# Row gradients as full-array block-diagonal products, fixed tiles for column vectors, gathered gradient tails, and a new order, in a planned attention-and-MLP gradient kernel

## The chip, the cores and the metric

The kernel runs on one core of a Trainium2 chip. A core has five engines with an instruction queue each: TensorE (PE, with its weight loads shown apart as PEld), VectorE (DVE), ScalarE (ACT), GpSimd (POOL) and SyncE (SP), and 16 DMA engines that move data between HBM and the on-chip memory SBUF. PE writes its products to PSUM; ACT and DVE copy them from there to SBUF, and a DMA stores them. The metric is the device time of one execution in microseconds (us). Before the change it is 470.13 us, the median of three runs (469.51 to 470.38).

## The reference

One token for each of two batch rows passes a layer norm, then attention over a cache of 4,096 positions and, in parallel, a gated bilinear MLP. The kernel computes the output and the gradients of all inputs but one:

```python
xn = _layernorm(x)                                   # (2, 1, 576)
q = xn @ wq                                          # 32 query heads of 128
scores = einsum("bhqd,bhkd->bhqk", q, k) * Dh**-0.5  # 16 cache heads, two query heads on each
o = softmax(scores) @ v
A = o @ wo
B = ((xn @ w_gate) * (xn @ w_up)) @ w_down           # 576 -> 4608 -> 576
out = x + A + B
_out, _vjp = jax.vjp(_f, A_x, A_k_cache, A_v_cache, A_wq, A_wo, B_w_gate, B_w_up, B_w_down)
return (_out, *_vjp(grad_out))
```

All arrays are bfloat16. The outputs are `out_0` (the result), `out_1` (gradient of x), `out_2` and `out_3` (gradients of the k and v caches, 32 MB each), `out_4` (of wq, 576 x 4096), `out_5` (of wo, 4096 x 576), `out_6` and `out_7` (of w_gate and w_up, 576 x 4608) and `out_8` (of w_down, 4608 x 576). With one token and a batch of two, every weight gradient is a sum of two outer products, and every cache gradient is one outer product for each pair of query heads. There is therefore little arithmetic for each byte: 92.5 MB are read and 92.5 MB are written.

## The kernel before

**Tiling.** Caches are worked on in 16 steps, each with two of the 16 cache heads and one batch row; each step loads two 1 MB buffers of k (t = 0) and two of v (t = 1). Weights are worked on in groups of 512 columns or rows: 8 groups for wq and wo, 9 slices for the MLP. All the large data goes through 16 SBUF buffers called `big` (128 partitions x 4,096 bfloat16), shared by cache loads (`kv`, at most 6), turned copies (`X`, 10), stores (`st`, 5) and the MLP's two weights (`G`, 2). PSUM gives three double-bank tiles `o` for outer products and two banks `m` for everything else.

**One step.** A loaded cache buffer is turned on DVE in 32 x 32 blocks (`t32`, L465), multiplied with the query (`score`, L1267), and passes softmax or its gradient. The probabilities are spread, and `contract` (L1441) sums the cache rows. GpSimd builds a block-diagonal tile `BD` (L1255) from a query or gradient vector, and `head_outer` (L1289) multiplies it with the spread probabilities: four products-and-copies of 1,024 columns fill one 1 MB store. The copy from PSUM is `cp`, on ACT (L469) or on DVE (L471).

**Weight gradients.** Three helpers make them, each through `unit` (take an `o` tile, multiply, copy to a store buffer, set an event) and `put` (wait for the events, start the store on SP, L695):

- Rows (`rows_unit`, `rows_outer`, L720 to L741) serve `out_5` and `out_8`. A vector tile `t` holds four blocks of 32 partitions that stand for four sets of gradient rows. Each of four units issues eight products of 32 partitions by 32 by 288 columns, one for each quadrant of the array, and one copy of 576 columns. Its event, on which `hb` or `R` is given back, comes when all four copies are done.
- Columns (`wide_unit`, `wide_outer`, L756 to L785, and `cols_unit` for a single slice) serve the first 512 rows of `out_4`, `out_6` and `out_7`, for three or four slices at a time. Each slice's vectors lie in a ring tile of their own (`D`, five of them; `Q`, six), so that a unit issues one product of 128 columns for each slice and each of two row groups.
- Tails (`tail_outer`, L813 to L835) serve rows 512 to 575, one slice at a time, through two small buffers `tl`: two copies of 256 columns, and a store of 64 rows of 1,024 bytes for each output.

**The order.** No order is written out by hand. All parts are Python generators, and the class `Order` plays them against estimated costs: at each turn it lets the part with the best due time go on, and the instructions come out in that sequence. Due times come from `pr(name, s)`: a step width, a constant for each kind of work (`PR`), corrections for the first and last steps (`HEAD`, `TAIL`) and one for each kind and step (`OFF`). `MLP_AT`, `WQ_AT` and `WO_AT` say behind which cache load the weights' loads come. So every engine's sequence is fixed when the kernel is built. SP issues all loads and nearly all stores in one sequence, and a store at its head that waits for a copy holds back every transfer behind it.

Of the kernel before, what the change touches and what calls it, by code (L numbers as in the profile page):

```python
# [13 lines left out]
P = 128  # L14
# [236 lines left out]
def DVE(cost):  # L251
    return ("op", "DVE", cost)
# [38 lines left out]
def DMA(engine, cost, nbytes, row=8192):  # L291
# [6 lines left out]
CAP = {"kv": 6, "X": 10, "st": 5, "G": 2}  # L298
OFF = {"mload": {0: 271.6, 1: -102.6, 2: -55.0, 3: -1.2, 4: 302.0, 5: -37.8, 6: -3.1, 7: -261.9, 8: -10.9, 10: 33.1,
       11: 0.8, 12: -207.4, 13: 133.1, 14: -7.7, 15: 159.7}, "wload": {0: 133.7, 1: 303.1, 2: 22.2, 3: 90.3,  # L300
# [7 lines left out]
       11: 190.3, 12: -28.6, 13: -116.3, 14: -697.9, 15: 68.4}, "load": {0: 14.2, 1: -78.4, 2: 45.7, 3: 100.8,  # L308
       4: -197.6, 5: 28.3, 6: 554.3, 7: 177.4, 8: 2.5, 9: -143.0, 10: -2.3, 11: -21.3, 12: 8.4, 13: -73.3, 14: 100.6,
       15: -142.0}, "front": {0: -179.7, 1: 85.4, 2: -277.2, 3: -256.2, 4: 1826.5, 5: 49.9, 6: 24.7, 7: 68.7,  # L310
       8: 74.6, 9: -133.5, 10: 299.2, 12: -72.9, 14: -82.2}, "turn0": {0: -74.5, 1: 12.8, 2: -59.7, 4: -98.2,
       5: -13.7, 6: 27.8, 7: -195.0, 8: 25.3, 9: -324.6, 10: 62.5, 11: 150.3, 12: 36.5, 13: 374.6, 14: 6.0,
       15: 40.1}, "con": {0: -246.4, 1: 1581.7, 2: 912.6, 3: -19.4, 4: -192.0, 5: -376.3, 6: -83.8, 8: 66.8,
       9: -106.8, 10: 1369.4, 12: 147.6, 13: 65.7, 14: 198.1, 15: 79.0}, "W0": {0: 31.7, 1: -255.2, 2: 62.9,
       3: -322.1, 4: -90.7, 5: -152.2, 6: 579.2, 7: -124.9, 8: 27.6, 9: -89.0, 10: -18.9, 11: -62.1, 13: 324.8,
       14: 5.0, 15: 14.0}, "back": {0: -32.5, 1: 35.1, 2: -23.7, 3: -119.2, 4: 97.7, 5: 800.9, 6: -2327.5, 9: -276.5,
# [3 lines left out]
       9: -447.4, 10: 31.8, 11: -210.3, 12: -58.4, 13: -249.2, 14: -11.7, 15: 118.0}, "dsc": {0: -165.3, 2: -11.7,  # L320
       3: -436.2, 4: 52.6, 5: -31.9, 7: 88.0, 8: -832.8, 9: 9.9, 10: -27.9, 12: -325.8, 14: 576.3, 15: -5.7},
       "mlp": {0: 894.9, 1: 15.9, 3: -552.7, 4: -163.6, 5: -290.8, 6: 30.0, 7: -24.7, 9: -5.3, 10: -0.7, 11: -155.0,
       12: -3.1, 13: 1.8, 14: 185.9, 15: 66.1}, "att": {0: 223.1, 1: 245.8, 2: -323.8, 4: 2.7, 5: -249.3, 7: -26.2,
       8: -319.6, 9: -120.7, 10: -196.9, 11: -385.5, 12: -86.1, 13: 62.5, 14: 3.3, 15: -375.0}, "conv": {1: 35.5,
       2: 158.9, 3: 36.7, 4: 96.9, 5: -12.0, 6: 28.4, 7: 88.3, 9: 84.0, 10: 537.9, 11: -9.1, 12: -109.0, 13: 291.0,
       14: 0.9, 15: 65.7}}
MLP_AT = [1.54, 11.84, 12.88, 7.42, 26.87, 116.29, 33.85, 48.49, 96.78]
WQ_AT = [-22, 9, 14, 22, 14, 17, 46, 47]
WO_AT = [-45, -45, -9, -46, 33, 37, 23, 31]
# [6 lines left out]
HEAD = {"turn0": -123.1, "turn1": -2289.3, "att": -2854.2, "dsc": -818.2, "con": 709.7, "out1": -2234.5,  # L336
        "out0": 965.3, "front": 1154.9, "back": -1312.3, "W0": 566.4, "W1": -1455.9, "BD1": 458.6, "BD0": 2899.0,
        "conv": -1146.6, "load": -3357.2}
TAIL = {"turn0": 905.5, "turn1": 2241.7, "att": -614.0, "dsc": -353.2, "con": 2724.6, "conv": 1530.3, "out1": 5670.9,
        "out0": -405.8, "front": -274.2, "back": 1989.7, "W1": 1283.8, "BD1": -1838.9, "BD0": -790.0, "load": 134.3,  # L340
        "W0": 1916.8}
PR = {"turn0": 854.2, "turn1": 1429.3, "att": -2428.5, "dsc": -1571.7, "conv": 280.9, "con": -1020.5, "out1": 3897.0,
      "out0": 1865.4, "front": 130.7, "back": 822.0, "W0": -2573.1, "W1": 268.5, "BD1": 2424.3, "BD0": -1416.8,
      "mlp": -908.1, "wout": -411.3, "store": -2408.5, "load": -294.1, "wload": -4334.0, "fin": -803.5,
      "const": 5061.6, "mload": -1458.5}
# [8 lines left out]
def kernel(  # L354
# [63 lines left out]
    tl_t = tiles("tl", 2, [P, FS])  # L418
# [4 lines left out]
    D_t = tiles("D", 5, [P, 2, P])  # L423
# [11 lines left out]
    Q_t = tiles("Q", 6, [P, P])  # L435
# [5 lines left out]
    for i in range(2):  # L441
        ch_t.append(dict(
            mx=const.tile([P, 1], FP32, name=f"mx{i}"), m4=const.tile([1, 4], FP32, name=f"m4{i}"),
            mr=const.tile([1, P], FP32, name=f"mr{i}"),
            negb=const.tile([P, 1], FP32, name=f"negb{i}"), ex=const.tile([P, P], FP32, name=f"ex{i}"),
            z=const.tile([P, 1], FP32, name=f"z{i}"), rz=const.tile([P, 1], FP32, name=f"rz{i}"),
            pr=const.tile([P, P], BF16, name=f"pr{i}"), cs=const.tile([P, 1], FP32, name=f"cs{i}"),
            cr=const.tile([P, 1], FP32, name=f"cr{i}"), ds=const.tile([P, P], BF16, name=f"ds{i}"),
            sp=const.tile([P, 2 * P], BF16, name=f"sp{i}")))

# [48 lines left out]
    xi = filled("xi", [2, 2, P], BF16, 0.0)  # L499
# [20 lines left out]
    mask16 = const.tile([P, 16], BF16, name="mask16")  # L520
    fold = const.tile([P, 4, GH], BF16, name="fold")
# [7 lines left out]
    def consts():  # L529
# [22 lines left out]
        yield DVE(0.45)  # L552
        sums(Q4[:], [[32, 4], [1, 32]])
        nc.vector.tensor_copy(mask8[:], view(Q4[:], 0, P, 0, [[1, 4], [0, 2]]))
# [12 lines left out]
    xnb = const.tile([2, D], BF16, name="xnb")  # L567
# [30 lines left out]
    def front():  # L598
# [16 lines left out]
        nc.vector.tensor_scalar(xnb[:], xb, mv[:, 0:1], rstd[:], op0=ALU.subtract, op1=ALU.mult)  # L615
# [4 lines left out]
        nc.vector.tensor_copy(view(xi[:], 0, 2, 0, [[P + 1, 2], [2, 64]]), view(xnb[:], 0, 2, 512, [[0, 2], [1, 64]]))  # L620
# [99 lines left out]
    def rows_unit(j, t, st):  # L720
        A, k = divmod(j, 2)

        def mms(o):
            for aa in range(2):
                for q in range(4):
                    nc.tensor.matmul(o[32 * q:32 * q + 32, aa, 0:HD2], lhsT=view(t, 32 * q, 32, 2 * A + aa, [[4, 32]]),  # L726
                                     rhs=dyr[32 * q:32 * q + 32, k * HD2:(k + 1) * HD2], start=True, stop=True)

        def ev(e, o):
            cp(e, view(st[:], 0, P, 2 * A * D + k * HD2, [[D, 2], [1, HD2]]), o[:, :, 0:HD2])  # L730
        return mms, (0.12, 0.208), D, ev

    def rows_outer(t, dst, p, event):
        i = yield ACQ("st")
        st, done = st_t[i], events(FC)
# [5 lines left out]
        yield SET(event)  # L741
# [14 lines left out]
    def wide_unit(rhss, dc, A, st, off):  # L756
        n = len(rhss)

        def mms(o):
            for j, rhs in enumerate(rhss):  # L760
                for aa in range(2):
                    a = 2 * A + aa
                    nc.tensor.matmul(o[:, aa, j * P:(j + 1) * P], lhsT=xnr[32 * a:32 * a + 32, dc * P:(dc + 1) * P],  # L763
                                     rhs=rhs(a), start=True, stop=True)
# [4 lines left out]
        return mms, (0.053 * n, 0.052 * n), 2 * P * n, ev  # L769

    def wide_outer(rhss, dst, p, event):
        width, last = FS * len(rhss), []
# [14 lines left out]
    def release(tag, slots, wait):  # L787
        yield WAIT(*wait)
        for i in slots:
            yield REL(tag, i)  # L790
# [801 lines left out]
```

## Time and profile before

| | |
|---|---|
| median of three runs | 470.13 us (469.51 to 470.38) |
| profiled execution: span from first to last instruction | 465.4 us (the profile gives no other time for it) |
| PE, DVE, ACT, POOL busy | 372.3, 372.8, 333.6, 143.2 us |
| data moved, mean rate | 185.97 MB, 400 GB/s |
| DMA issues | 26 of 64 KB from `tl`, 17 of 576 KB, 74 of 1 MB and 5 of 512 or 768 KB from `big`, 2 of the result rows; the rest are loads |
| mean granted TensorE clock | 0.715 |

"Busy" is the time in which an engine executed something; copies that overlap at their ends count once. The page cuts the span into 40 slices and gives for each how busy the DMA engines were and how many GB/s they moved. A group of instructions is named by its line, engine, operation and the tiles that it writes and reads; its row gives the busy time, the mean of one instruction in ns, and the idle time of its engine just ahead of it, with what ended that idle time. In the list of SP's waits the three numbers are the sum in us, how many waits, and the longest one.

### The profile page before, as it was taken

The numbers are of one execution on the slowest core, as the hardware profiler recorded it, in microseconds if no ns is written. First come the engines' busy times: TensorE is split into PE (matmuls) and PEld (weight loads), VectorE is DVE, ScalarE is ACT, GpSimd is POOL, SyncE is SP. The second block draws the span as 40 slices with busy tenths as digits, with TensorE's granted clock in tenths as the row PEclk, the third lists the DMA queues.
The fourth block names the chain that finished last, engine by engine and source line by source line (L and its number), as shares of the span: only waits on it lengthen the run. The fifth ranks groups of instructions, "written<-read, shape, count | busy, mean of one in ns | idle before, by whom it ended". The sixth has DMA issues, their size and how long they took to land.

```text
span 465.4 us, 15712 instructions
## 1 busy us (share of the span) xinstructions
PE 372.3 (80%) x6750; PEld 213.0 (46%) x6750; DVE 372.8 (80%) x711; ACT 333.6 (72%) x512; POOL 143.2 (31%) x174
## 2 busy tenths in 40 slices
PE   1688779888987777888788877789788978977886
PEld 1545355546443344455555354455424533544443
DVE  8887888878779787879887778788878866877883
ACT  3268638969986687675777775678778968687874
POOL 0740042403407343470015341600743316033200
PEclk9997675877776677677775696756866665677865
DMA  8999999999999999999999999999999999999995
GB/s 316 414 410 420 411 421 387 417 416 373 371 422 422 405 424 406 420 420 421 413 407 419 419 417 404 400 350 374 418 422 424 418 411 424 423 359 390 422 368 207
DMA packets 40710, 185.97 MB, mean 400 GB/s; under 512 B 3640, under 2 KB 12352, under 8 KB 24256
## 3 DMA queue, kind: packets, MB, share of 16 engines
q1 hardware_dynamic: 40632, 184.96, 98.7%
q8 instruction: 53, 0.87, 0.7%
q14 instruction: 17, 0.14, 0.1%
q10 hardware_dynamic: 8, 0.00, 0.0%
HBM read 92.48 MB, written 92.48 MB: 397 GB/s over the span
## 4 chain that ended last, share of the span: by engine, by line
DMA 35%; PE 20%; ACT 10%; DVE 10%; issue 5%; SPq 1%; DVEq 0%; ACTq 0%
DMA out_dram<-big 20%; DMA big<-in_A_v_cache_dram 15%; ACT big L469 8%; DVE big L465 6%; PE ps_o L1289 4%; PE ps_m L1441 3%; PE ps_m L1267 3%; PE ps_o L726 2%; DVE big L471 2%; PE ps_o L763 1%; PE ps_m L677 1%; SPq L1197 1%; PE ps_m L887 1%; ACT pr L1357 0%; PE ps_o L1539 0%
## 5 line engine op out<-in xcount | busy, mean ns | idle before, releaser
L469 ACT CAST big<-ps_o 128x1024 bf16<-128x1024 f32 (+2 forms) x303 | 272.5, 957 | 51.0 <-PE ps_o L1289 31.4
L465 DVE STREAM_TRANSPOSE big<-big 128x1024 f32<-128x1024 f32 x146 | 176.3, 1223 | 21.6 <-DMA big<-in_A_v_cache_dram 10.1
L1255 POOL TENSOR_TENSOR BD<-vr,mask 128x2048 bf16<-128x2048 bf16 x32 | 115.3, 3603 | 118.6 <-PE ps_o L1289 42.9
L471 DVE CAST big<-ps_o 128x1024 bf16<-128x1024 f32 (+1 forms) x75 | 81.3, 1086 | 15.6 <-PE ps_o L1289 5.9
L1267 PE MATMUL ps_m<-big,W 128*32 128x128 bf16 x2048 | 60.2, 281 | 5.4 <-issue 3.5
L1232 POOL COPY W<-rep 32x16 bf16<-32x16 bf16 x128 | 24.5, 192 | 116.7 <-DVE rep L1006 95.8
L1267 PEld LDWEIGHTS <-W 128*32 128x32 bf16 x2048 | 47.0, 125 | 24.8 <-issue 23.7
L1289 PE MATMUL ps_o<-BD,pp 32*128 32x512 bf16 x256 | 46.1, 495 | 12.9 <-ACT big L469 7.2
L1289 PE MATMUL ps_o<-BD,dd 32*128 32x512 bf16 x256 | 43.6, 499 | 9.9 <-ACT big L469 7.8
L465 DVE STREAM_TRANSPOSE big<-ww 128x1152 f32<-128x1152 f32 (+1 forms) x25 | 33.0, 1319 | 2.4 <-DMA out_dram<-big 1.1
L1441 PE MATMUL ps_m<-big,pp 128*32 128x512 bf16 x256 | 31.9, 582 | 3.5 <-DVE pp L465 3.2
L1441 PE MATMUL ps_m<-big,dd 128*32 128x512 bf16 x256 | 28.3, 533 | 1.7 <-DVE dd L465 1.4
L1289 PEld LDWEIGHTS <-pp 32*128 32x128 bf16 x256 | 10.2, 97 | 33.2 <-issue 24.6
L1289 PEld LDWEIGHTS <-dd 32*128 32x128 bf16 x256 | 10.5, 98 | 24.8 <-issue 16.9
L1038 POOL COPY qr<-qd 128x256 bf16<-128x256 bf16 x8 | 3.2, 396 | 54.2 <-DVE qd L471 43.8
L726 PE MATMUL ps_o<-dyr,R 32*32 32x288 bf16 x256 | 18.0, 401 | 1.6 <-ACT big L469 1.5
L763 PEld LDWEIGHTS <-xnr 32*128 32x128 bf16 x368 | 12.5, 117 | 10.7 <-issue 9.2
L726 PE MATMUL ps_o<-dyr,hb 32*32 32x288 bf16 x288 | 15.5, 330 | 1.3 <-ACT big L469 1.2
L887 PE MATMUL ps_m<-big,Wdy 128*128 128x128 bf16 x162 | 15.0, 265 | 0.2
L763 PE MATMUL ps_o<-D,xnr 32*128 32x128 bf16 x256 | 13.3, 276 | 2.3 <-ACT big L469 1.7
L677 PE MATMUL ps_m<-big,wm 128*32 128x128 bf16 x416 | 13.4, 290 | 1.5 <-DVE qd L992 0.8
L1451 ACT ACTIVATE osb<-ps_m 128x512 bf16<-128x512 f32 x15 | 9.0, 597 | 7.9 <-PE ps_m L1441 7.7
(205 smaller groups left out, 483.8 us busy)
## 6 DMA issues: line engine op xcount, KB each, us to landing
out_dram<-big SPq DMA_DIRECT2D x74, 1024.0 KB, 14.0
big<-in_A_k_cache_dram SPq DMA_DIRECT2D x32, 1024.0 KB, 14.4
big<-in_A_v_cache_dram SPq DMA_DIRECT2D x32, 1024.0 KB, 12.6
out_dram<-big SPq DMA_DIRECT2D x17, 576.0 KB, 10.7
ww<-in_B_w_down_dram SPq DMA_DIRECT2D x9, 576.0 KB, 12.2
ww<-in_A_wo_dram SPq DMA_DIRECT2D x8, 576.0 KB, 7.4
ww<-in_A_wq_dram SPq DMA_DIRECT2D x8, 512.0 KB, 12.4
big<-in_B_w_gate_dram SPq DMA_DIRECT2D x4, 1024.0 KB, 14.6
```

The lines of the kernel that those rows point to most:

```text
L465: nc.vector.transpose(out, in_)
L469: nc.scalar.copy(out, in_)
L471: nc.vector.tensor_copy(out=out, in_=in_)
L677: nc.tensor.matmul(dp[32 * q:32 * q + 32, 0:P], lhsT=W, rhs=view(X, 0, P, xoff(q, s), [[FS, 4], [2, 32]]), start=(s == 0), stop=(s == S - 1))
L726: nc.tensor.matmul(o[32 * q:32 * q + 32, aa, 0:HD2], lhsT=view(t, 32 * q, 32, 2 * A + aa, [[4, 32]]), rhs=dyr[32 * q:32 * q + 32, k * HD2: ...
L763: nc.tensor.matmul(o[:, aa, j * P:(j + 1) * P], lhsT=xnr[32 * a:32 * a + 32, dc * P:(dc + 1) * P], rhs=rhs(a), start=True, stop=True)
L887: nc.tensor.matmul(dh, lhsT=Wdy[:, e, 2 * k:2 * k + P], rhs=view(X[:], 0, P, 64 * k + e, [[D, FC], [2, 32]]), start=(k == 0 and e == 0), s ...
L1232: nc.gpsimd.tensor_copy(view(W_t[t][w][:], 32 * a, 32, 6 + 8 * a, [[G * WW, 4], [WW, G], [1, 2]]), view(rep_t[grp[g]["qs"]][:], 32 * a, 32 ...
L1255: nc.gpsimd.tensor_tensor(BD_t[i][:], view(vr_t[v][:], 0, P, 0, [[0, 16], [1, Dh]]), view(mask16[:], 0, P, 0, [[1, 16], [0, Dh]]), ALU.mult)
L1267: nc.tensor.matmul(sc[32 * cq:32 * cq + 32, :], lhsT=view(W[:], 0, P, (be * G + l) * WW + 6 - 4 * c2 - 2 * l, [[1, 32]]), rhs=view(X[:], 0 ...
L1289: nc.tensor.matmul(o[:, k, :], lhsT=pr2[32 * c4:32 * c4 + 32, :], rhs=BD[32 * c4:32 * c4 + 32, 8 * l + 4 * h2:8 * l + 4 * h2 + 4, :], star ...
L1441: nc.tensor.matmul(ct[32 * j:32 * j + 32, :], lhsT=view(rT, 0, P, 4 * c + 2 * l, [[1, 32]]), rhs=kv_t[kvS[s][t][l]][:, Dh * c:Dh * (c + 4) ...
```

## The change

- **Rows.** GpSimd expands the vector tile into `RB`, a tile of 4 x 128 columns in which each block of 32 partitions keeps only its own 32 columns and is zero elsewhere (a product with the mask `maskq`). One product over all 128 partitions then gives what took four quadrants before. The row gradient is treated as one flat stretch of 2,304 columns that is cut at 1,024 and 2,048 for the copies, and for the products also at multiples of 512 and 576: 3, 4 and 1 products and one copy each. The event that gives `hb` or `R` back now comes behind `RB`'s construction.
- **Columns.** The ring tiles `D` and `Q` become fixed tiles `Dm` (nine slices) and `Qm` (eight groups). Slices lie side by side, so one product covers up to four of them. Nothing is given back any more.
- **Tails.** They are gathered: MLP slices 0 to 3 and 4 to 8 for both outputs, groups 0 to 3, 4 to 6 and 7 for `out_4`. They take an `st` buffer of `big` instead of `tl`, and a store has rows of 1,024 bytes for each slice gathered.
- **Memory.** To make room, the helper tiles `xi`, `xnb` and `mr` lie inside `Dm` and `sp`.
- **Order.** All constants of `pr`, `OFF`, `HEAD`, `TAIL`, `MLP_AT`, `WQ_AT`, `WO_AT`, and also `BIAS` and `SLACK`, have new values, so every engine's sequence is new. The last cache loads, for example, have 24 transfers behind them on SP instead of 25.

```diff
-BIAS = 0.186
-SLACK = {"PE": 0.09, "ACT": 0.26, "DVE": 0.4, "POOL": 5392037994838238.0, "SP": 5703748027825.79}
+BIAS = 0.255
+SLACK = {"PE": 0.03, "ACT": 0.26, "DVE": 0.37, "POOL": 10000.0, "SP": 10000.0}
...
-    tl_t = tiles("tl", 2, [P, FS])
-    D_t = tiles("D", 5, [P, 2, P])
+    RB_t = tiles("RB", 2, [P, 4, P])
+    Dm = const.tile([P, NFS, 2, P], BF16, name="Dm")
+    Qm = const.tile([P, NG, P], BF16, name="Qm")
-    Q_t = tiles("Q", 6, [P, P])
...
-    def rows_unit(j, t, st):
-        A, k = divmod(j, 2)
+    def rows_unit(RB, lo, hi, st):
+        cuts = sorted({lo, hi} | {x for x in range(lo, hi) if x % FS == 0 or x % D == 0})
 
         def mms(o):
-            for aa in range(2):
-                for q in range(4):
-                    nc.tensor.matmul(o[32 * q:32 * q + 32, aa, 0:HD2], lhsT=view(t, 32 * q, 32, 2 * A + aa, [[4, 32]]),
-                                     rhs=dyr[32 * q:32 * q + 32, k * HD2:(k + 1) * HD2], start=True, stop=True)
+            flat = o[:].rearrange("p a n -> p (a n)")
+            for x, y in zip(cuts, cuts[1:]):
+                c, n = divmod(x, D)
+                nc.tensor.matmul(flat[:, x - lo:y - lo], lhsT=RB[:, c, :], rhs=dyr[:, n:n + y - x], start=True, stop=True)
...
     def rows_outer(t, dst, p, event):
+        b = yield ACQ("RB")
+        RB = RB_t[b]
+        yield POOL(0.95)
+        nc.gpsimd.tensor_tensor(RB[:].rearrange("p c (q m) -> p c q m", q=4), view(t, 0, P, 0, [[1, 4], [0, 4], [4, 32]]),
+                                view(maskq[:], 0, P, 0, [[0, 4], [1, 4], [0, 32]]), ALU.mult)
+        yield SET(event)
...
-        for j in range(FC):
-            yield SPAWN(unit(*rows_unit(j, t, st), done[j]), p)
+        for u in range(3):
+            yield SPAWN(unit(*rows_unit(RB, 1024 * u, min(1024 * u + 1024, FC * D), st), done[u], kind="f"), p)
...
-    def wide_unit(rhss, dc, A, st, off):
+    def wide_unit(n, rhs, dc, A, st, off):
         def mms(o):
-            for j, rhs in enumerate(rhss):
-                for aa in range(2):
-                    a = 2 * A + aa
-                    nc.tensor.matmul(o[:, aa, j * P:(j + 1) * P], lhsT=xnr[32 * a:32 * a + 32, dc * P:(dc + 1) * P],
-                                     rhs=rhs(a), start=True, stop=True)
+            for aa in range(2):
+                a = 2 * A + aa
+                nc.tensor.matmul(o[:, aa, 0:n * P], lhsT=xnr[32 * a:32 * a + 32, dc * P:(dc + 1) * P],
+                                 rhs=rhs(a), start=True, stop=True)
...
-    def tail_outer(rhss, dsts, p, event, w0=0):
-        i = yield ACQ("tl")
+    def tail_outer(n, rhss, dsts, p):
+        i = yield ACQ("st")
+        st, parts = st_t[i], [(j, min(j + 4, n)) for j in range(0, n, 4)]
...
+    BUNCH, TAILS = ((0, 1, 2, 3), (4, 5, 6, 7), (8,)), ((0, 1, 2, 3), (4, 5, 6, 7, 8))
```

More of the change, by code (lines that the diff above doesn't have):

```diff
@@ L566 @@
     xy = const.tile([2, 2 * D], BF16, name="xy")
-    xnb = const.tile([2, D], BF16, name="xnb")
+    xnb = view(Dm[:], 0, 2, 0, [[1, D]])
     bst = const.tile([2, 2, 6], FP32, name="bst")
@@ L828, in ev @@
             def ev(e, o):
-                r = slice(64 * w0, 64 * (w0 + nw))
-                cp(e, st[r, 256 * A:256 * A + 256].rearrange("p (a f) -> p a f", a=2), o[r, :, 0:P])
-            return mms, (0.053, 0.104), 256, ev
-        for A in range(2):
-            yield SPAWN(unit(*mk(A), done[A]), p)
-        yield WAIT(*done)
-        yield SET(event)
+                r = slice(0, 64 * nw)
+                cp(e, view(st[:], 0, 64 * nw, FS * j0 + 2 * P * A, [[P, 2], [FS, j1 - j0], [1, P]]),
+                   o[r, :, 0:P * (j1 - j0)].rearrange("p a (j f) -> p a j f", j=j1 - j0))
@@ new lines, in mk, with bunch_outer @@
+            return mms, (0.053 * (j1 - j0), 0.052 * nw), 2 * P * (j1 - j0), ev
+        for k, (j0, j1) in enumerate(parts):
+            for A in range(2):
+                yield SPAWN(unit(*mk(A, j0, j1), done[2 * k + A]), p)
+    def bunch_outer(gs, p):
+        g0, g1 = gs[0], gs[-1] + 1
+        if len(gs) > 1:
+            yield SPAWN(wide_outer(g1 - g0, lambda a: Qm[32 * a:32 * a + 32, g0:g1, :], out_4[0:512, g0 * FS:g1 * FS], p), p)
+        else:
+            yield SPAWN(cols_outer(lambda a: Qm[32 * a:32 * a + 32, g0, :], out_4[0:512, g0 * FS:g1 * FS], p, Event()), p)
+        yield SPAWN(tail_outer(g1 - g0, [lambda a, j0, j1: Qm[32 * a:32 * a + 32, g0 + j0:g0 + j1, :]],
+                               [out_4[512:576, g0 * FS:g1 * FS]], p), p)
@@ new lines, with grads @@
+    BUNCH, TAILS = ((0, 1, 2, 3), (4, 5, 6, 7), (8,)), ((0, 1, 2, 3), (4, 5, 6, 7, 8))
+    dE = [Event() for _ in range(NFS)]
+    def grads(ks, p):
+        yield WAIT(*[dE[k] for k in ks])
+        k0, k1 = ks[0], ks[-1] + 1
+        for w, out in enumerate((out_6, out_7)):
+            dst = out[0:512, k0 * FS:k1 * FS]
+            if len(ks) > 1:
+                yield SPAWN(wide_outer(k1 - k0, lambda a, w=w: Dm[32 * a:32 * a + 32, k0:k1, w, :], dst, p), p)
+            else:
+                yield SPAWN(cols_outer(lambda a, w=w: Dm[32 * a:32 * a + 32, k0, w, :], dst, p, Event()), p)
@@ L837, in free_gu, with tail_grads @@
+    def tail_grads(ks, p):
+        yield WAIT(*[dE[k] for k in ks])
+        k0, k1 = ks[0], ks[-1] + 1
+        yield SPAWN(tail_outer(k1 - k0, [lambda a, j0, j1, w=w: Dm[32 * a:32 * a + 32, k0 + j0:k0 + j1, w, :] for w in range(2)],
+                               [out[512:576, k0 * FS:k1 * FS] for out in (out_6, out_7)], p), p)
     def free_gu(sl):
@@ L904, in mlp @@
         yield SPAWN(rows_outer(hb[:], out_8[f0:f0 + FS, :], po, E[0]), po)
-        yield SPAWN(tail_outer([lambda a, w=w: D2[32 * a:32 * a + 32, w, :] for w in range(2)],
-                               [out[512:576, f0:f0 + FS] for out in (out_6, out_7)], po, dE[i][1]), po)
-        for ks in BUNCH:
-            if i == ks[-1]:
-                yield SPAWN(grads(ks, po), po)
+        for todo, kss in ((grads, BUNCH), (tail_grads, TAILS)):
+            for ks in kss:
+                if i == ks[-1]:
+                    yield SPAWN(todo(ks, po), po)
         yield DVE(0.31)
```

160 lines of the change are left out of this document (65 added, 95 removed), and 21 rows, old and new, of the table OFF.

## The prediction

> **What bounds the kernel now.** I read the page's busy shares and DMA queue first, then the DMA queue's own waits, then stretches of the span, then the groups of instructions by shape.
>
> The page:
>
> ```profile
> PE 372.3 (80%) x6750; PEld 213.0 (46%) x6750; DVE 372.8 (80%) x711; ACT 333.6 (72%) x512; POOL 143.2 (31%) x174
> ...
> DMA  8999999999999999999999999999999999999995
> GB/s 316 414 410 420 411 421 387 417 416 373 371 422 422 405 424 406 420 420 421 413 407 419 419 417 404 400 350 374 418 422 424 418 411 424 423 359 390 422 368 207
> ...
> q1 hardware_dynamic: 40632, 184.96, 98.7%
> ```
>
> The one DMA queue has packets under way for nearly the whole span, but a slice moves between 350 and 424 GB/s. The trace's packet records give the floor: taken at the median time of their size (309 ns for 8,192 bytes, 178 for 4,608, 159 for 4,096, 121 for 3,072, 46 for 1,024, 9 for the completion write that each DMA leaves on each of 16 engines), all data packets make 446.1 us of sixteen engines. The span is 465.4, so 19.3 us are lost. By the same records about 2.6 go at the start and 3 to 5 behind the last cache load; the remaining 11 or so lie between.
>
> The DMA queue's own waits, and five stretches (PE, PEld, DVE, ACT, POOL busy, clock, DMA share, GB/s):
>
> ```profile
> SPq L695 <- ACT big L469: 81.7, 48, 4.8
> SPq L695 <- DVE big L471: 79.6, 31, 5.9
> SPq L695 <- ACT tl L469: 20.9, 13, 4.2
> ...
> SPq L695 <- DVE tl L471: 2.3, 4, 0.7
> ```
>
> ```profile
> 340.00:350.00 10.00, 7.18 (x53) 2.32 (x49) 7.70 (x13) 8.26 (x11) 3.60 (x1) 0.67 1.01 425
> ...
> 105.00:130.00 25.00, 21.70 (x490) 12.84 (x482) 20.35 (x36) 24.30 (x34) 8.74 (x10) 0.77 0.98 376
> 285.00:330.00 45.00, 38.08 (x765) 23.06 (x757) 38.03 (x66) 32.67 (x49) 12.28 (x11) 0.69 0.99 379
> 405.00:430.00 25.00, 20.01 (x407) 11.28 (x408) 20.01 (x34) 19.54 (x32) 7.51 (x3) 0.72 1.00 379
> 430.00:465.40 35.40, 27.41 (x430) 14.66 (x417) 24.29 (x46) 23.43 (x33) 3.30 (x1) 0.68 0.84 333
> ```
>
> SP issues every transfer in one order, and its stores stand waiting for the copies from PSUM: 161 us behind `big`, 23 behind `tl`. Mostly nothing is lost, because transfers issued earlier are still moving. In the last four stretches, where weight gradients are written beside cache gradients, that stock runs out and the rate falls. So the bound is the DMA queue, and where it runs dry, the copies on ACT and DVE.
>
> **The change, part by part.** Durations:
>
> ```profile
> L469 ACT CAST big<-ps_o 128x1024 bf16<-128x1024 f32 x247 | 238.0, 1022 | 37.2 <-PE ps_o L1289 31.4 <-PE ps_o L763 1.9 <-DMA out_dram<-big 1.9
> L469 ACT CAST big<-ps_o 128x576 bf16<-128x576 f32 x48 | 29.5, 644 | 12.6 <-PE ps_o L726 12.1
> ...
> L469 ACT CAST tl<-ps_o 128x256 bf16<-128x256 f32 x14 | 5.0, 379 | 1.2 <-PE ps_o L825 1.2
> ```
>
> ```profile
> L471 DVE CAST big<-ps_o 128x1024 bf16<-128x1024 f32 x55 | 66.3, 1209 | 9.4 <-PE ps_o L1289 5.9 <-PE ps_o L763 1.8 <-issue 1.6
> ...
> L471 DVE CAST big<-ps_o 128x576 bf16<-128x576 f32 x20 | 14.9, 747 | 6.3 <-PE ps_o L726 4.8 <-ACT big L469 1.3 <-issue 0.2
> ```
>
> ```profile
> L1255 POOL TENSOR_TENSOR BD<-vr,mask 128x2048 bf16<-128x2048 bf16 x32 | 115.3, 3603 | 118.6 <-PE ps_o L1289 42.9 <-ACT vr L469 38.8 <-DVE vr L471 31.3
> ```
>
> *Tails, transfers.* 26 stores of 64 rows of 1,024 bytes become seven: two of 64x4,096 and two of 64x5,120 for `out_6` and `out_7`, and 64x4,096, 64x3,072 and 64x1,024 for `out_4`. Packets: 1,664 x 46 ns / 16 = 4.78 us before; after, (192 x 159 + 128 x 197, estimated between the 4,608 and 8,192 rows, + 64 x 121 + 64 x 46) / 16 = 4.15. With 19 completion writes of 9 ns: -0.8 us. The queue is the bound, so this counts in full. SP also loses 19 issues of 0.47 us and the 17 `tl` waits; the store behind each is the next one late, so I count nothing for them.
>
> [...]
>
> *Tails, copies.* 34 copies of 256 columns (ACT 0.37 to 0.38, DVE 0.40 to 0.42 us: 13.1) become six of 1,024, two of 768 (0.815) and four of 256: 9.7. -3.4 us of ACT and DVE. The tail's buffer now comes from `big`: five more holdings among 96; no wait for such a buffer shows as a long one, so nothing, bounds 0 to +2 us (the longest SP wait for a `big` landing in that view, 3.0, once).
>
> *Rows.* Per gradient, four copies of 576 columns become two of 1,024 and one of 256. 17 gradients: 48 x 0.644 + 20 x 0.747 = 45.9 before; 43.3 after with the same split of engines. -2.5 us. PE: 544 products of 288 columns (33.5 us busy, four quadrants side by side) become 136 over all 128 rows, 39,168 columns in all. No row has that shape; the 32-row, 512-column products of L1289 (89.7 us for 512, two at a time) give 0.35 us per 512 columns, the column tiles of L1441 (60.2 for 512, four at a time) 0.47: 27 to 36 us. I take no change; PE is not what stores wait for longest.
>
> The new step is GpSimd's block-diagonal `RB`: 512 of the 2,048 elements of L1255, 0.90 us, 17 times. POOL is 69% idle and nobody is listed waiting for `BD`. It stands before the rows' products and before the `BD` and `W` builds queued behind it: 0 while that cover holds, at worst 17 x 0.9 = 15 us if each gradient waited in the open. I take 0, because the rows are low in the plan's priorities and other copies fill the time.
>
> *Wide columns.* 368 products of 128 columns (18.5 us) become 96 of up to 512; at L1289's 0.175 each, 17 us. The copies stay. -2 us on PE, hidden. The fixed tiles `Dm`, `Qm` take away waits for a free `D` or `Q`, of which the trace shows none: 0.
>
> Over the whole lists, with each shape at its mean here, ACT falls from 370.3 to 366.4 us and DVE from 410.7 to 408.3 (sums of records, which overlap: DVE's busy time is 372.8). Behind the first turn of the last loaded cache buffer, DVE has 30.7 us of records instead of 32.3, ACT 31.9 instead of 33.2.
>
> *The order.* It is wholly new, so its effect is bounded, not priced. Below: the 11 us lost in the middle could nearly all go, -9. Above: the new order asks more of DVE early. Ahead of the cache store at packet position 105 us stand 100.4 us of DVE records, against 87.3 ahead of the one at 101 before; at 161 us it is 153.6 against 145.9; at 300 the two are about level. DVE was idle 18 us of the first 105 (86.74 busy), which covers the first; uncovered, the second is +7.7. I take 0, as that idle time is the nearest row.
>
> *Sum.* Last cache load: its packet position moves from 405.0 to 404.5, -0.5. Behind it: half a per-engine saving each, the mean of 1.6 and 1.3, -1.4. In the middle: the remaining 3.4 us of copies are 1.7 per engine, and I count half, as the dry stretches hold only part of the gradients: -0.9. Total -2.8: span 462.6. The page gives the profiled execution its span alone; the median of the runs, 470.13, lies 4.7 above it, and I keep that: **467.3**.
>
> **Rivals.** About 0.2% (0.94 us) is what a measurement of this kernel can tell from no change.
>
> *A. The order brings more.* The dry stretches of 285 to 330 and 405 to 430 go too. For it: those stretches are about balance, and work on every engine falls. Against: SP's store waits are everywhere. Six of the bound's nine: 461.
>
> *B. Only the packets count.* The copies saved lie where the queue is full: -0.8, 469.3. For it: in most slices the queue is already at 420.
>
> *C. Slower: DVE early.* If DVE's early work is not covered, stores between positions 97 and 165 come late and the DMA runs dry: up to +7.7 on -2.8, 475. It decides once more than 2.8 us of the demand is uncovered. For it: 12 us more are asked by 105 us. Against: DVE's idle 18 us there.
>
> [...]
>
> **How the numbers follow.** Forecast 0.43 (its own range 464 to 469), A 0.20, B 0.14, C 0.19, D 0.04. Faster is the forecast and A, 0.63; B is the same, 0.14; C and D slower, 0.23. 460.5 to 473.5 reaches past A and two thirds into C, which leaves out the end of either.
>
> **What would show it.** [...] Copies: no 576 form; ACT's wait for rows, 12.1 us, not larger. POOL near 158 us, still without waiters. Tail: less than 43 us from the first turn of the last loaded cache buffer to the end. Order: if C, GB/s falls between 95 and 170 us; if A, 285 to 330 moves more than 400. Wrong altogether if rows wait for `RB` in the open, or if PE's full-array products outrun its slack and copies wait for L726's successor.

## The result, and the profile after

The changed kernel takes 467.32 us (median of six runs, 466.03 to 468.62), against 470.25 us of the kernel before beside it (six runs, 469.40 to 471.70): a ratio of 0.9937, with a 95% interval from 0.9916 to 0.9957. In a second, longer comparison (twelve runs and 29 runs, e5 below) it is 467.36 against 469.22 us, 0.9966 (0.9949 to 0.9984). Taken together the change gains between 1 and 3 us. The forecast was 467.3 us; what follows shows that its sum came out right although several of its terms did not.

The page of the changed kernel, its busy shares, its DMA rows in 40 slices, and the DMA queue:

```profile
PE 364.8 (78%) x6001; PEld 203.9 (44%) x6002; DVE 370.5 (79%) x707; ACT 329.1 (70%) x478; POOL 160.7 (34%) x191
...
DMA  8999999999999999999999999999999999999995
GB/s 314 413 409 415 418 423 394 401 386 343 400 417 411 410 412 372 420 423 422 421 415 412 414 406 413 397 367 364 418 423 426 422 426 423 384 350 416 421 380 221
...
q1 hardware_dynamic: 39112, 184.96, 98.6%
```

The queue is as full as before (98.6 against 98.7%). The tenth slice, 105 to 117 us, now moves only 343 GB/s. Packets taken at the median of their size make 448.5 us of sixteen engines, against 449.7 before, both with the instruction fetches (47 of 16 KB instead of 53); without the fetches it is 445.2 against 446.0. This profiled execution is the slowest of its six, with a span of 466.8 us; the others span 464.2 to 466.4.

SP's waits, and four stretches of the span (PE, PEld, DVE, ACT, POOL busy, granted clock, DMA share, GB/s):

```profile
SPq L700 <- ACT big L471: 107.6, 63, 8.2
SPq L700 <- DVE big L473: 100.5, 41, 8.9
SPq L1141 <- DMA out_dram<-big: 19.8, 13, 2.5
```

```profile
95.00:130.00 35.00, 31.55 (x508) 17.35 (x505) 25.90 (x51) 27.86 (x37) 11.38 (x13) 0.65 0.98 375
...
285.00:330.00 45.00, 36.34 (x622) 19.03 (x615) 38.65 (x66) 34.43 (x46) 11.54 (x9) 0.77 0.99 386
405.00:430.00 25.00, 22.00 (x365) 11.42 (x367) 21.58 (x34) 21.45 (x31) 11.82 (x4) 0.64 0.98 370
430.00:466.80 36.80, 27.28 (x380) 14.74 (x372) 22.74 (x47) 24.77 (x31) 1.04 (x1) 0.73 0.87 345
```

SP still stands before its stores until a copy ends: 208 us behind `big`, where it had been 161 behind `big` and 23 behind `tl`. The dry stretch of 285 to 330 us is hardly better here (386 against 379 GB/s), that of 405 to 430 is no better (370 against 379), and the one that lay between 105 and 130 us now begins at 95 and is deeper: from 95 to 115 us it is 357 GB/s, where it was 394. All this is one execution. The profile of e5, whose time is nearer the middle, has this in the same stretches, so two executions of the changed kernel differ there by as much as the change moved them:

```profile
95.00:130.00 35.00, 31.40 (x504) 16.86 (x502) 26.15 (x50) 28.02 (x35) 11.52 (x13) 0.65 1.00 384
285.00:330.00 45.00, 32.58 (x590) 17.32 (x577) 38.95 (x67) 35.25 (x47) 12.97 (x7) 0.78 1.00 397
405.00:430.00 25.00, 20.41 (x335) 10.53 (x334) 21.79 (x35) 20.36 (x29) 11.82 (x4) 0.66 1.01 385
```

The groups that the change touches:

```profile
L471 ACT CAST big<-ps_o 128x1024 bf16<-128x1024 f32 x279 | 269.4, 1030 | 36.7 <-PE ps_o L1288 30.0 <-PE ps_o L771 2.4 <-PE ps_o L732 2.2
...
L742 POOL TENSOR_TENSOR RB<-hb,maskq 128x512 bf16<-128x512 bf16 x9 | 9.4, 1043 | 5.9 <-DVE hb L883 5.6
...
L742 POOL TENSOR_TENSOR RB<-R,maskq 128x512 bf16<-128x512 bf16 x8 | 8.3, 1042 | 58.9 <-ACT R L471 37.9 <-DVE R L473 20.9
```

The 576-column copies are gone, ACT waits 2.2 us for rows (12.1 before), and `RB` takes 1.04 us each.

### The profile page after: what moved, and what is told of

Same layout as the page of the kernel before. It is cut to its first block, busy times and chain, and to the rows that moved or that the text cites. A ratio compares the mean times of both kernels' runs of the same rounds, so it can differ in the third digit from the quotient of the medians.

```text
span 466.8 us, 14164 instructions
## 1 busy us (share of the span) xinstructions
PE 364.8 (78%) x6001; PEld 203.9 (44%) x6002; DVE 370.5 (79%) x707; ACT 329.1 (70%) x478; POOL 160.7 (34%) x191
## 3 DMA queue, kind: packets, MB, share of 16 engines
q1 hardware_dynamic: 39112, 184.96, 98.6%
## 4 chain that ended last, share of the span: by engine, by line
DMA 40%; PE 21%; ACT 11%; DVE 7%; issue 3%; POOL 1%; SPq 0%; ACTq 0%; DVEq 0%; POOLq 0%
DMA out_dram<-big 23%; DMA big<-in_A_v_cache_dram 14%; ACT big L471 9%; DVE big L467 5%; PE ps_o L1288 4%; PE ps_m L1440 3%; DMA ww<-in_B_w_down_dram 3%; PE ps_m L1266 2%; PE ps_o L732 2%; PE ps_m L896 1%; PE ps_m L1027 1%; PE ps_o L771 1%; POOL BD L1254 1%; DVE big L473 1%; PE ps_m L682 1%
## 5 line engine op out<-in xcount | busy, mean ns | idle before, releaser
L471 ACT CAST big<-ps_o 128x1024 bf16<-128x1024 f32 (+3 forms) x294 | 277.5, 1010 | 37.0 <-PE ps_o L1288 30.0
L473 DVE CAST big<-ps_o 128x1024 bf16<-128x1024 f32 (+2 forms) x79 | 82.5, 1048 | 11.1 <-PE ps_o L732 3.4
L1266 PE MATMUL ps_m<-big,W 128*32 128x128 bf16 x2048 | 56.9, 271 | 6.9 <-DVE hb L883 2.5
L732 PE MATMUL ps_o<-dyr,RB 128*128 128x512 bf16 (+7 forms) x135 | 30.7, 370 | 4.0 <-ACT big L471 3.4
L742 POOL TENSOR_TENSOR RB<-R,maskq 128x512 bf16<-128x512 bf16 x8 | 8.3, 1042 | 58.9 <-ACT R L471 37.9
L732 PEld LDWEIGHTS <-RB 128*128 128x128 bf16 x136 | 13.5, 119 | 13.7 <-issue 11.5
L1027 PE MATMUL ps_m<-big,Wdy 128*128 128x128 bf16 x144 | 14.6, 280 | 6.0 <-DVE Dm L902 3.0
L1027 PEld LDWEIGHTS <-Wdy 128*128 128x128 bf16 x144 | 13.3, 128 | 9.2 <-issue 6.8
L1341 ACT COPY sp<-m 1x128 f32<-1x128 f32 x16 | 4.7, 294 | 17.8 <-DVE m L1339 17.8
L896 PE MATMUL ps_m<-big,Wdy 128*128 128x128 bf16 x162 | 14.4, 258 | 3.4 <-DVE oT L1460 1.8
L471 ACT CAST osb<-ps_m 128x512 bf16<-128x512 f32 x15 | 8.8, 586 | 10.2 <-PE ps_m L1440 10.2
```

The costliest lines, as they stand in the source:

```text
L471: nc.scalar.copy(out, in_)
L473: nc.vector.tensor_copy(out=out, in_=in_)
L732: nc.tensor.matmul(flat[:, x - lo:y - lo], lhsT=RB[:, c, :], rhs=dyr[:, n:n + y - x], start=True, stop=True)
L742: nc.gpsimd.tensor_tensor(RB[:].rearrange("p c (q m) -> p c q m", q=4), view(t, 0, P, 0, [[1, 4], [0, 4], [4, 32]]), view(maskq[:], 0, P, ...
L896: nc.tensor.matmul(dh, lhsT=Wdy[:, e, 2 * k:2 * k + P], rhs=view(X[:], 0, P, 64 * k + e, [[D, FC], [2, 32]]), start=(k == 0 and e == 0), s ...
L1027: nc.tensor.matmul(dp, lhsT=Wdy[:, e, 2 * k:2 * k + P], rhs=view(X[:], 0, P, 64 * k + e, [[D, GH], [2, 32]]), start=(k == 0 and e == 0), s ...
```

## The experiments

"The changed kernel" in these runs is the one of e5. e6 to e8 ran beside e5, and their distance from it is the difference of the means. The others did not, and their distance is the difference of the mean ratios to the kernel before, which ran beside all of them (469.1 to 469.5 us). All distances have 95% intervals from the spread of the runs. In e1, e2, e6 to e8 and e10 to e12 the planner's costs are untouched, so that every engine's order is that of the changed kernel.

### e5: the changed kernel again

> The changed kernel as it is, beside the next three on the same chip, so that their differences to it can be read from one call. 467.3 us, or 0.9937 of the kernel before.

467.36 us (465.97 to 469.91), 0.9966 (0.9949 to 0.9984) of before. One line of comment moves its line numbers up by one.

### e1 and e12: the products as before

```diff
-                nc.tensor.matmul(flat[:, x - lo:y - lo], lhsT=RB[:, c, :], rhs=dyr[:, n:n + y - x], start=True, stop=True)
+                for q in range(4):
+                    r = slice(32 * q, 32 * q + 32)
+                    nc.tensor.matmul(flat[r, x - lo:y - lo], lhsT=view(RB, 32 * q, 32, c, [[4, 32]]), rhs=dyr[r, n:n + y - x],
+                                     start=True, stop=True)
...
-            yield SPAWN(unit(*rows_unit(RB, 1024 * u, min(1024 * u + 1024, FC * D), st), done[u], kind="f"), p)
+            yield SPAWN(unit(*rows_unit(t, 1024 * u, min(1024 * u + 1024, FC * D), st), done[u], kind="f"), p)
```

This is e1, without the instruction that builds `RB`. In e12, also:

```diff
-                nc.tensor.matmul(o[:, aa, 0:n * P], lhsT=xnr[32 * a:32 * a + 32, dc * P:(dc + 1) * P],
-                                 rhs=rhs(a), start=True, stop=True)
+                for j in range(n):
+                    nc.tensor.matmul(o[:, aa, j * P:(j + 1) * P], lhsT=xnr[32 * a:32 * a + 32, dc * P:(dc + 1) * P],
+                                     rhs=rhs(a)[:, j], start=True, stop=True)
```

and the tails' products in the same way.

> The changed kernel in the same order of all engines, with the row products made as before the change: four 32-row products, one for each quadrant of the array, instead of one block-diagonal product, and no RB on GpSimd; the copies of 1,024 and 256 columns stay. My theory (the form of the product is neutral, the fewer copies count): 467.3 us, within 0.7; POOL busy falls by 17.7 us to about 143; ACT's wait for rows stays near 2.2 us. Rival (the full-array product is what ended the 12.1 us of waiting for rows, so it carries the gain): ACT's wait for rows goes back to about 10 us and the time to 469 or 470 us.

> The changed kernel in the same order with all products as before the change: rows by quadrants without RB, and wide columns and tails one slice of 128 columns at a time (some 270 and 40 products more). The prediction counted the products as 0: 467.4 us. e1 alone (rows by quadrants) stood 1.2 us above the changed kernel, over two calls; if that is real this lies at 468.6 to 469.5.

e1: 468.76 us, 0.9992 (0.9973 to 1.001) of before, 1.3 +- 1.0 us above e5. e12: 469.45 us, 0.9999 (0.9985 to 1.0013) of before, 1.7 +- 0.9 us above e5. With all other parts of the change in place and only the products undone, nothing of the gain is left (e12 lies 0.0 +- 0.7 us from the kernel before). So, within the new order, the term that the prediction put at 0 is the largest one. Two limits: the order was planned for the costs of the new products, and no run gives the old ones an order of their own; and the products alone were not put into the kernel before.

How it acts is not in the profile. The busy shares of e5, of e12 and then of e1, with its row of ACT's copies:

```profile
PE 365.7 (79%) x6002; PEld 206.2 (44%) x6002; DVE 370.8 (80%) x707; ACT 329.4 (71%) x478; POOL 160.7 (35%) x191
```

```profile
PE 367.8 (79%) x6750; PEld 214.5 (46%) x6750; DVE 370.6 (79%) x707; ACT 329.3 (70%) x478; POOL 143.3 (31%) x174
```

```profile
PE 359.0 (77%) x6410; PEld 201.2 (43%) x6410; DVE 371.0 (79%) x707; ACT 328.7 (70%) x478; POOL 143.6 (31%) x174
...
L471 ACT CAST big<-ps_o 128x1024 bf16<-128x1024 f32 x279 | 268.8, 1030 | 39.2 <-PE ps_o L1289 33.9 <-PE ps_o L734 2.3 <-PE ps_o L772 2.0
```

PE is busy 2.1 us longer in e12 and 6.7 us less in e1 than in e5. Neither figure says much: e2, e6 and e8 below have e5's products, and in their profiled executions PE is busy for 369.8, 358.5 and 356.0 us. The rows' products take 31.7 us of PE in e5, and in e1, by quadrants, 15.4 + 15.0. ACT's wait for rows, which e1's expectation named as the sign of the rival, stayed at 2.3 us. So the rival's size was right and its sign did not show: the fall from 12.1 to 2.2 us came with the order or the copies, not with the form of the product. What else differs in e12 is 748 weight loads and as many products (8.3 us of PEld) and six instruction fetches of 16 KB; each of those takes one engine about 0.95 us, some 0.4 us of sixteen together. Which of these the 1.7 us go through is left open.

### e2: RB built twice

```diff
+        nc.gpsimd.tensor_tensor(RB[:].rearrange("p c (q m) -> p c q m", q=4), view(t, 0, P, 0, [[1, 4], [0, 4], [4, 32]]),
+                                view(maskq[:], 0, P, 0, [[0, 4], [1, 4], [0, 32]]), ALU.mult)
```

> The changed kernel with each RB built twice in a row on GpSimd, nothing else: 17 x 1.04 = 17.7 us more on POOL (160.7 to 178). My theory (RB is covered, since rows stand low in the priorities): 467.3 us, no change within 0.5. Rival (rows wait for RB in the open in part of the 17 gradients): 1.04 us for each that does, so 472 us if a quarter do, 476 if half do.

467.72 us, 0.9971 (0.9952 to 0.999), 0.3 +- 1.1 us above e5, with 17.7 us more on POOL:

```profile
PE 369.8 (79%) x6002; PEld 207.6 (45%) x6002; DVE 371.0 (80%) x707; ACT 328.7 (71%) x478; POOL 178.4 (38%) x208
```

`RB` is covered, at its measured 1.04 us as at the predicted 0.90: a quarter of the gradients in the open would have made 4.4 us.

### e3 and e4: the constants of the order exchanged

Only the block of constants from `CAP` to `PR` changes places: e3 has the new structure with the old one, e4 the old structure with the new one.

> The changed structure with all constants of the order from before (due times, gates, bias, slack). The prediction counted the new order as 0 and the structure as -2.8 us: by that 467.4 us. Rival (the new order carries the gain): 470.2 or more. A third: constants fit only the structure that they were made for, then this is slower than both, above 472.

> The structure from before with all constants of the new order. By the prediction's count (order 0): 470.2 us. Rival (the order carries the gain): 467.5. Third (constants fit only their own structure): above 472.

e3: 479.95 us, 1.0221 (1.0197 to 1.0245) of before. e4: 481.26 us, 1.0251 (1.0216 to 1.0287). The third expectation holds: neither set of constants fits the other structure, and 12 us, many times the effect of the change, lie between a fitting order and one that doesn't fit. In e3 the packets lose 7.3 us between 95 and 130 us and 4.3 between 130 and 165, against 2.9 and 0.3 in e5. "The new order alone" is therefore no quantity that can be measured here, and the prediction's 0 for it is neither shown nor refuted. Nor does either run say what the new structure would do under an order made for it by the old planner settings.

### e6: the row copies in four pieces

```diff
-            cp(e, st[:, lo:hi], o[:].rearrange("p a n -> p (a n)")[:, 0:hi - lo])
+            for c0 in range(lo, hi, 256):
+                cp(e, st[:, c0:c0 + 256], o[:].rearrange("p a n -> p (a n)")[:, c0 - lo:c0 - lo + 256])
```

> The changed kernel in the same order, but each of the 34 row copies of 1,024 columns is made as four copies of 256 by the same engine: by the shapes' means 0.48 us more each (4 x 0.377 - 1.03), 16 us more of ACT and DVE together, mostly ACT. The prediction's rule (half of a per-engine share, because the dry stretches hold only part of the gradients) counted 3.4 us of copies in the middle as 0.9: 16 us would be 4.3, so 471.6 us. Rival (the copies lie where the queue is full): 467.3. Another rival (stores wait for copies everywhere, so they count in full): 475 or more.

467.87 us, 0.9973 (0.9954 to 0.9992), 0.3 +- 1.0 us above e5. But the dose was not 16 us. ACT's busy time rose from 329.4 to 334.8 us for 99 copies more, 55 ns each, and DVE's did not rise:

```profile
PE 358.5 (77%) x6002; PEld 199.7 (43%) x6002; DVE 370.5 (80%) x710; ACT 334.8 (72%) x577; POOL 160.7 (35%) x191
```

The timeline of ACT shows why (start, length, and how many in a row): first four copies of 1,024 columns in the kernel before, then eight of 256 in e6:

```profile
367.16 3.76 ACT L469 CAST big<-ps_o 128x1024 bf16<-128x1024 f32 x4 [0.90 <-PE ps_o L1289]
```

```profile
63.26 2.31 ACT L471 CAST big<-ps_o 128x256 bf16<-128x256 f32 x8 [0.41 <-PE ps_o L732]
```

Four copies whose records are 1.02 us each take 3.76, not 4.08; eight of 0.41 take 2.31, not 3.3. The records of neighbouring copies overlap: where they stand in a row, it is 904 ns from one start to the next for 1,024 columns, 535 for 576 and 264 for 256 on ACT (mean records: 1,022, 644, 370 to 417), and about 1,132 and 330 ns on DVE for 1,024 and 256 (1,209 and 404 to 423). A further copy in a row costs ACT 0.05 us, not the 0.16 that a sum over records gives it. The 5.4 us that were added cost at most 1.3 us; the prediction's whole term (2.3 us of time for 5.9 us of copies) would have made 2.1 of them.

### e7: the gathered tails in pieces

```diff
-            nc.sync.dma_start(d, x)
+            for c0 in range(0, row // 2, cut or row // 2):
+                nc.sync.dma_start(d[:, c0:c0 + cut] if cut else d, x[:, c0:c0 + cut] if cut else x)
```

with `cut=FS` for tails.

> The changed kernel in the same order, with each gathered tail stored as one transfer of 64 rows of 1,024 bytes for each slice, 26 instead of 7, out of the same buffer. By the prediction: 19 more completion writes and shorter packets, +0.8 us, counted in full: 468.1 us; the packets' own sum rises from about 447.5 to 448.3. Rival (lost time elsewhere covers it): 467.3, no change. Rival (SP's 19 further issues of about 0.4 us hold back the transfers behind them): 469 or more.

473.75 us (473.53 to 473.83), 1.0102 (1.0083 to 1.0122) of before, 6.2 +- 0.6 us above e5: the last rival. The packets' sum rises by 0.8 us, as reckoned (448.5 to 449.3, with the fetches at their own median). The rest is where SP's issues leave the DMA without work. Five microseconds near the end, in e7 and then in e5 (same columns as above):

```profile
450.00:455.00 5.00, 4.39 (x38) 2.10 (x33) 3.62 (x8) 4.39 (x6) 0.00 (x0) 0.66 0.29 75
```

```profile
450.00:455.00 5.00, 4.78 (x50) 2.11 (x49) 3.46 (x7) 4.49 (x6) 0.00 (x0) 0.50 0.94 355
```

and the transfers that SP issues in e7 between 440 and 460 us (how many, KB each, us to landing):

```profile
out_dram<-big SPq DMA_DIRECT2D x11, 64.0 KB, 3.9
```

```profile
SPq L701 <- ACT big L471: 3.7, 3, 3.0
SPq L701 <- DMA out_dram<-big: 2.5, 3, 0.9
```

The last fence is e7's list of SP's waits from 442 to 456 us (sum in us, how many, the longest). Ten tail stores, whose data was complete at 444.0 us, go out one after the other from 443.8 to 454.9. An issue of a 64-row store takes SP 0.47 to 2.2 us there (8.8 us for the ten), and three times it waits besides (2.5 us) for the transfer eight places ahead of it to land. In the traces before and after, SP's transfers take eight completion semaphores in turn (220 of 221 and 201 of 202 have that of the eighth ahead), and none of the 111 and 100 for which the traces give the eighth's landing starts before it, while 37 and 21 start before the seventh has landed: the theory that e9's expectation names. A 64 KB store needs only 0.2 us of the sixteen engines, so a bunch of them leaves the DMA empty: 75 GB/s, where e5 moves 355. The same happens at 135 us, where eight stand together (31 to 167 GB/s between 134 and 137 us, where e5 moves 372 to 429).

### e8: less turning early

```diff
+                        if h and s in (3, 4):
+                            continue
                         t32(pairs(X_t[x][:, 2048 * h:2048 * h + 2048]), pairs(src[:, 2048 * h:2048 * h + 2048]))
```

> The changed kernel in the same order without the second half of the turn of the eight cache buffers of steps 3 and 4 (the products that read it use what lies in the buffer): 8 x 1.22 = 9.8 us less of DVE between about 60 and 125 us of the span. If DVE's early demand is what makes the DMA run dry there (the prediction's rival C), most of the 3.7 us lost between 95 and 130 comes back: 464 us. If something else is late there (the products, ACT's copies, the buffers), the loss stays above 3 and the time at 467.3. A run to come takes the same turns away in steps 7 and 8, where nothing is lost.

467.70 us, 0.9971 (0.9954 to 0.9989), 0.2 +- 1.0 us above e5, though DVE is busy 9.1 us less:

```profile
PE 356.0 (76%) x6002; PEld 202.3 (43%) x6002; DVE 361.7 (78%) x699; ACT 328.8 (71%) x478; POOL 160.7 (34%) x191
```

The packets do lose less between 95 and 130 us, 1.5 against 2.9, but more behind it: 3.6 against 2.3 from 130 to 190. So DVE's early work has a part in where the DMA runs dry, and none that shows in when the kernel ends. The counterpart in steps 7 and 8 was not made, since there was no gain to tell apart.

### e9 and e10: both kernels without their tail stores

```diff
-            nc.sync.dma_start(d, x)
+            if tag != "tl":
+                nc.sync.dma_start(d, x)
```

and likewise for the tails of the changed kernel.

> The kernel before the change without its 26 tail stores (the copies into their buffers stay; rows 512 to 575 of three outputs are not written). The packets' price is 4.8 us and 0.2 of completion writes: 469.2 - 5.0 = 464.2 us if a small transfer costs only its packets, as the prediction took it. Theory after e7: SP has eight completion semaphores, and a transfer waits for the eighth one ahead of it, so a 64 KB transfer takes the place of 1 MB; 19 such transfers in bunches cost 5.6 us above their packets in e7, here they stand one or two at a time, so a part of that: 460 to 463 us.

> The changed kernel in the same order without its 7 tail stores (same remark). Packets: 4.2 us, so 467.4 - 4.2 = 463.2 us. With e9: if the gathering of tails carries the gain by more than its packets, the two kernels without tails lie less than 1.1 us apart (1.9 in the last call, less 0.8 of packets), near 0 if it carries all of it; if it is worth its packets alone, they stay 1.1 apart.

e9: 464.96 us (463.64 to 468.96), 0.9905 (0.9881 to 0.9929). e10: 462.42 us (462.15 to 462.75), 0.9854 (0.9834 to 0.9874). In the kernel before, 26 tails cost 4.5 +- 1.1 us by the ratio, which is their packets (5.0) and no more than about half a microsecond for SP: there they stand one or two at a time. In the changed kernel seven cost 5.2 +- 0.8 us, a little over their packets (4.2). Without any tail store the two kernels still lie 2.5 +- 1.5 us apart, so the gain does not come from the gathering of the stores; the gathered copies are still made in e10.

### e11: half the scores

```diff
-        for be in range(4):
+        for be in range(2):
...
-                        start=(l == 0 and be == 0 and c2 == 0), stop=(l == G - 1 and be == 3 and c2 == 1))
+                        start=(l == 0 and be == 0 and c2 == 0), stop=(l == G - 1 and be == 1 and c2 == 1))
```

> The changed kernel in the same order with half of the score products left out (two of the four channel groups, so scores are of half the channels): about 28 us less of PE in 64 places, everything else as it is. e6 (16 us more of copies) and e8 (9.8 us less of DVE) changed nothing, so it is not those engines that the dry stretches wait for. If PE's products stand in the chain from load to store there, this gives 464 us or less; if PE has slack too and the chain is one of hand-overs and of SP's slots, 467.4.

466.58 us, 0.9934 (0.991 to 0.9957), 1.5 +- 1.2 us below e5. This run doesn't tell what it was made for, because most of the products that are left run longer (487 to 541 ns in the costliest group), at a lower granted clock (0.67 against 0.73). e11's page and its costliest group of outer products, and then the same group of e5:

```profile
PE 363.0 (78%) x4977; PEld 190.4 (41%) x4978; DVE 370.8 (80%) x707; ACT 330.5 (71%) x478; POOL 160.5 (34%) x191
...
L1288 PE MATMUL ps_o<-BD,dd 32*128 32x512 bf16 x256 | 50.7, 541 | 9.1 <-ACT big L471 4.5
```

```profile
L1289 PE MATMUL ps_o<-BD,dd 32*128 32x512 bf16 x256 | 45.9, 487 | 12.4 <-ACT big L472 6.6 <-DVE big L474 2.4 <-DVE dd L468 2.0
```

A thousand products fewer, and PE is busy 363.0 us instead of e5's 365.7, in one execution each. The scores themselves went from 58.4 to 34.9 us, but the outer products from 487 to 541 ns each in the group shown. The mean granted clock is 0.657 to 0.677 in the six runs, and 0.706 to 0.755 in the twelve of e5.

## Why the prediction was right, and where it was not

The forecast was 2.8 us of gain; 2.9 us were measured beside it, and 1.7 +- 0.7 (of the means) in the longer comparison. Step by step:

- **Tails, transfers (-0.8, of which the sum took -0.5 ahead of the last cache load).** The packets' sum fell by 1.2 us, 0.8 of it here and the rest in six instruction fetches, and e9 and e10 show that tails cost about their packets in both kernels. The 0.8 itself is below what two runs can tell apart. That SP's 19 issues count for nothing holds for the places where the kernel before had them; e7, 6.2 us for 0.8 of packets, shows that it does not hold everywhere.
- **Copies (-0.9 in the middle, part of -1.4 at the end).** The work was judged about rightly, and its worth was not. By the means of their records, 34 tail copies and 68 row copies were to be 5.9 us less (the sum took 6.3, from the whole lists of ACT and DVE, without saying what else changes). Records overlap; in busy time, which counts overlaps once, the copies into the store buffers fell by 2.5 us on ACT (280.0 to 277.5) and 2.5 on DVE (85.0 to 82.5). If all of them stood in unbroken rows on ACT, the distances from start to start would give only 1.1 for the tails and 1.2 for the rows. For the time, e6 is the measure: 5.4 us more of copying cost at most 1.3 us. At that rate the 5.0 us saved are worth 0 to 1.2, where the prediction took 2.3.
- **The end (-1.4).** Not seen. From the first turn of the last loaded cache buffer to the end it is 43.1 us in the profile before, 43.1 in the one after and 43.4 in e5; "less than 43" was the sign.
- **Products (0).** "I take no change; PE is not what stores wait for longest" is the step that failed: in the new order they are worth 1.7 +- 0.9 us (e12), most of it the rows by the middle values (e1). The rows' busy time was judged rightly, 30.7 us within the 27 to 36 given, but the step from there to "no change" did not hold. Why it did not is open.
- **`RB` (0.90 us, covered).** Right on the cover (e2), and 1.04 us instead of 0.90: a quarter of the elements costs 29% of L1255's 3.60.
- **Buffers and fixed tiles (0).** The longest waits for `Dm` after the change are 3.0 us of PE in the profile after and 3.8 in e5, once each, and none is longer than 0.5 for `Qm`; nothing in the runs tests the term alone.
- **The order (0, between -9 and +7.7).** Can't be taken apart from the structure (e3, e4). Its lower bound was too wide: the 11 us lost in the middle were reckoned without the instruction fetches, whose 53 packets of 0.97 us take 3.2 us of the sixteen engines; with all packets some 7 us are lost between 60 and 430 us.
- **The profiled execution (4.7 us from span to median).** Wrong. In all runs of e5 the time is 1.8 us above the span (1.74 to 1.84). The 465.4 us of the profile before are an unusually short span: of 69 spans of the kernel before in the later comparisons, with a mean of 467.2, one is as short. So the predicted span of 462.6 us was not met either (464.2 to 466.8 in the six runs). The prediction kept the difference, and that the sum came out right all the same is luck in this step: the error of the span was carried on both sides of it. For the kernel before, the time lies 2.1 us above the span on average (1.8 to 3.0), so 0.3 us of the gain lie outside the span; the prediction did not reckon with that, and no run says why.

So 467.3 was right as a sum, and what carries it is not settled. Take the mean span less the sum of all packets, which is what the DMA loses: 17.5 us in the kernel before (467.2 less 449.7), 17.2 in e5 (465.7 less 448.5), and 18.6 in e12 (467.5 less 448.9). Seen from the kernel before, the span is 1.4 us shorter, and 1.2 of it are packets. Seen from e12, it is 1.8 us shorter, and only the form of the products differs. Both hold, because e12 loses 1.1 us more than the kernel before: the new order, copies and tiles cost about that with the old products. Each of these figures is good to some 0.7 us, so this last one is barely clear of the noise, and no run shows the old products under an order of their own. Neither view leaves room for much of the 2.3 us that the prediction took for the copies.

Of the rivals, A failed by its own sign (386 GB/s, and 397 in e5, not over 400). B, only the packets, would be a ratio of 0.998: outside the first comparison's interval and at the edge of the second's, so it is too small, but as the larger part of the gain it is not excluded. C was right about the place: GB/s fell between 95 and 115 us, and the packets lose 3.7 us between 95 and 130 (2.9 in e5), where it was 2.3. Its "12 us more" are 13.1 by the prediction's own two figures (100.4 less 87.3), for stores 4 us apart. It was wrong about the price, since e8 takes that demand away without a gain. D, the 0.04 for stores of 64 rows whose packets come slower than others of their size, is a term that no run shows. In the profile before, the 56 packets of 1,024 bytes between 365 and 370 us, which are a tail's, took 46 ns, the median of their size in the whole kernel. In the one after, the 640 of 4,096 bytes between 126 and 138 us, 128 of them from the 64-row stores issued at 125.0 and 126.4, had a median of 159 ns, and 13 took longer than 165. The 128 of 5,120 bytes at the end had a median of 196 (197 estimated); 33 of them took longer than 200 and 23 took 300 or more. So the medians are those that the sum took.

## What to carry to other kernels

Price a small copy that stands in a row by the distance from start to start, not by the mean of its records: the two differ by 0.11 us a copy here (e6). And check the saving against the engine's busy time, which counts overlaps once. Where two kernels have two orders made by a planner, undo the parts one at a time within one order; exchanging the orders measures only the fit (12 us). Before a median is compared with a profile, ask how that one execution stands among the others: here its span lay 1.8 us under the mean. And a part that is undone in the changed kernel measures its worth there, beside the other parts; it need not be what the change has gained by it.

## What the runs showed that was not expected

- Half of the score products removed (23.5 us of them), and PE's busy time fell by 2.7 us between the two profiled executions: the mean granted clock went from 0.73 in e5's twelve runs to 0.67 in e11's six. No run here shows why the clock was lower with fewer products.
- SP needs 0.47 us and more, up to 2.2, to issue a store of 64 rows of 1,024 bytes in e7, whose packets take 0.2 us of the sixteen engines. Ten in a row emptied the DMA (75 GB/s) and, with the smaller bunches ahead of them, cost 5 us above their packets; the 26 that the kernel before spreads out cost no more than theirs, within about 1 us.
- Splitting the rows' products into quadrants, and the wide ones into slices, costs 1 to 2 us of 467 in the new order (1.3 +- 1.0 and 1.7 +- 0.9), though ACT's wait for rows does not show it.
